# Two edits of one kernel: the first output product in nine blocks of 512 tokens, and attention bursts ahead of their tick's product

## The chip, the cores and the metric

The kernel runs on one core of a Trainium2 chip. The metric is the device time of one execution in microseconds (us), median of the runs shown. TensorE (PE) does the matmuls, VectorE (DVE), ScalarE (ACT) and GpSimd (POOL) the element-wise work, and SyncE (SP) issues every transfer, in one queue in the order of the program. Each engine works off its own instructions strictly in order.

## The reference

Three layers, one behind the other. Everything is float32, but the weights of the two feed-forward layers come as float64.

```python
# 1. retention: batch 8, heads 8, sequence 576, head size 64
scores = (q @ k.T) / sqrt(64)
attn = (scores * Dmat) @ v          # Dmat[i, j] = gamma_h ** (i - j) for i >= j, else 0
x = attn as [4608 tokens, 512]
# 2. maxout layer, width 768
h = maximum(maximum(x @ w1, x @ w2), x @ w3)
z = h @ w_out                       # [4608, 512]
# 3. bilinear layer, width 1024
g = (z @ w1') * (z @ w2')
out = (g @ w3') @ w_out'            # [4608, 512]
```

## The kernel before, in words

Every matmul of layers 2 and 3 is made of three: an operand is split into a high half that the fast float32r form holds exactly and a low half (`copy_r` on ACT makes the high half, `low` on DVE or POOL subtracts it), and high x high, low x high and high x low are summed in PSUM.

**Layers 1 and 2 in one stage.** The 4608 tokens are nine blocks of 512 (`N1`). Everything in this stage is put into a list with `when(t, fn)` and issued in the order of `t`; equal times keep the order of entry, and attention is entered ahead of the products. One block is 18 ticks (`T_BLK`): one product of 12 matmuls (`products`, L349, tile `ps_h`) at each tick k, entered at k - 0.5. Attention of one chunk of 64 or 128 tokens consists of the scores (`sc`, L263), the state's update (`st`, L288) and the outputs (`o`, L276 and L282), each in small float32 matmuls. For block t they are planned during block t - 1: outputs at `t_n`, the state's update 0.01 before, and the scores of the next chunk 0.01 after, with `t_n` = 18 (t - 1) - 0.5 + 18 i / (chunks in the block), which are four or five. So `t_n` falls on a product's time for the first chunk of a block, and for the third of four. At the same time the weights are turned from float64 and kept in DRAM. The first blocks' h goes to DRAM as `h_d`, one tensor for each block of 512.

**The first output product** (z = h @ w_out, tile `ps_z`, L506) works on blocks of 384 (`N2`), twelve of them. A block has six steps k; a step is 12 matmuls (four PSUM banks, three each) with one h tile (`hr` as loaded, `hh` and `hl` its halves), taken from the ring of `H_RING` tiles, and behind it in the program `split_h` prepares the tile two steps on and loads another (`load_h`; half of the loads come in two parts, since blocks of 384 and of 512 do not coincide). In four of the six steps one entry of `steps` is worked off: first the sums of weights for the next layer (L480, and splits), then weights for the w product. A block ends with four copies out of PSUM, two by ACT (L555) and two by DVE (L553), into one tile `zo`, which one DMA stores to `z_d`. The eight banks are two sets of four, so the next block runs while the copies are made.

**Then** come a product of two weights (`ps_w`), the bilinear layer (`ps_x`, `ps_v`, `ps_y`) in six pairs of 384-token blocks, which reads z back (`operands`, tile `zr`), and the last product.

Of the kernel before, what the change touches and what calls it, by code (L numbers as in the profile page):

```python
# [9 lines left out]
F32 = mybir.dt.float32  # L10
F32R = mybir.dt.float32r
I32 = mybir.dt.int32
U32 = mybir.dt.uint32
AF = mybir.ActivationFunctionType
# [5 lines left out]
NT, DM = B * S, H * D  # L20
F1, F2 = 768, 1024
G = H // 2
P = 128
N1 = 512
N2 = 384
KF1, KF2, KD = F1 // P, F2 // P, DM // P
# [43 lines left out]
def tile_retention_maxout_bilinear(ctx: ExitStack, tc, a, out):  # L70
    nc = tc.nc
    chunks = chunk_list()

    def copy_r(dst, src):
        nc.scalar.activation(dst, src, AF.Copy)  # L75

    def low(eng, dst, full, hi):
        eng.tensor_tensor(dst, full, hi.bitcast(F32), ALU.subtract)  # L78

    def load(dst, src):  # L80
        nc.sync.dma_start(out=dst, in_=src)  # L81
# [3 lines left out]
    dram = ctx.enter_context(tc.tile_pool(name="dram", bufs=1, space=DRAM))  # L85
# [2 lines left out]
    wo1_d = dram.tile([P, KF1, DM], F32, name="wo1_d")  # L88
    wp_d = dram.tile([P, 2, 2, KD, 512], F32, name="wp_d")
    h_d = [dram.tile([P, KF1, N1], F32, name=f"h_d{t}") for t in range(NT // N1)]  # L90
    z_d = [dram.tile([P, KD, N2], F32, name=f"z_d{t}") for t in range(NT // N2)]
    g_d = [dram.tile([P, KF2, N2], F32, name=f"g_d{t}") for t in range(NT // N2)]
    w4_d = dram.tile([P, KF2, DM], F32, name="w4_d")

# [21 lines left out]
    n_blk = NT // N1  # L116
    T_BLK = 3 * KF1
# [210 lines left out]
    for t, ns in by_block.items():  # L328
        for i, n in enumerate(ns):
            if t == 0:  # L330
                attend(n, CHUNK_AT[i], CHUNK_AT[i] + 2, CHUNK_AT[i] + 3)
            else:

                t_n = T_BLK * (t - 1) - 0.5 + T_BLK * i / len(ns)
                attend(n, behind + 0.01 if t > 1 else t_n - 3, t_n - 0.01, t_n)
                behind = t_n

# [28 lines left out]
    for t in range(n_blk):  # L366
        for f in range(KF1):
            for i in range(3):
                k = T_BLK * t + 3 * f + i
# [12 lines left out]
    zp = {}  # L382
    n2 = NT // N2
# [17 lines left out]
    def get_w1o(k):  # L401
        return splitter(zp["p"], wo1_d[:, k], *zp["w"][k], nc.vector if k % 2 else nc.gpsimd, "wr", 2)

    H_RING, H_AHEAD = 4, 4
    hq = dict(loaded=0, split=0)

    def load_h():
        n = hq["loaded"]
        if n < n2 * KF1:
            hq["loaded"] = n + 1  # L410
            j, k = divmod(n, KF1)
            raw = hq[n] = zp["p"].tile([P, N2], F32, tag="hr", name="hr", bufs=H_AHEAD)
            t0, done = j * N2, 0
            while done < N2:
                blk, off = divmod(t0 + done, N1)
                m = min(N1 - off, N2 - done)
                load(raw[:, done:done + m], h_d[blk][:, k, off:off + m])
                done += m

    def split_h():  # L420
        n = hq["split"]
        if n < n2 * KF1:
            hq["split"] = n + 1
            raw = hq.pop(n)
            hh = zp["p"].tile([P, N2], F32R, tag="hh", name="hh", bufs=H_RING)
            hl = zp["p"].tile([P, N2], F32R, tag="hl", name="hl", bufs=H_RING)
            copy_r(hh, raw)
            low(nc.vector if n % 2 else nc.gpsimd, hl, raw, hh)
            hq[n] = hh, hl
            load_h()  # L430
# [7 lines left out]
    for n in range(H_AHEAD):  # L438
        when(t_last + 11 + 0.5 * n, load_h)
    for n in range(2):  # L440
        when(t_last + 15 + n, split_h)

    with tc.manual_schedule():
# [7 lines left out]
        def bank8(name):  # L451
            return ps_8.tile([P, 512], F32, tag="b", name=name)
# [43 lines left out]
        steps = [groups[0][0]]  # L496
# [3 lines left out]
        def product(ps, terms, start=True, stop=True, again=False):  # L500

            mms = []
            for lh, ll, rh, rl in terms:
                mms += [(lh, rh), (ll, rh), (lh, rl)]
            for j, (l, r) in enumerate(mms):
                nc.tensor.matmul(ps, l, r, start=start and j == 0, stop=stop and j == len(mms) - 1, skip_group_check=again)  # L506
# [16 lines left out]
        def open_34():  # L523

            t34["p"] = t34x.enter_context(tc.tile_pool(name="t34", bufs=2, side="left"))
            gets = [lambda m=0, e=e: get_w3t(m, e) for e in range(2)] + [lambda k=k: get_wo2(k) for k in range(KF2)]
            gets += [lambda m=1, e=e: get_w3t(m, e) for e in range(2)]
            pending = []

            def step():  # L530
                if len(pending) == 3 or not gets:
                    pending.pop(0)()
                if gets:
                    pending.append(gets.pop(0)())

            return [step] * (len(gets) + 3)

        slots = (1, 2, 4, 5)
        for j in range(n2):
            zs = [bank8("ps_z") for _ in range(KD)]  # L540
            for k in range(KF1):
                h = hq.pop(j * KF1 + k)
                for m in range(KD):
                    ms = slice(m * P, (m + 1) * P)
                    wh, wl = zp["w"][k]
                    product(zs[m][:, :N2], [(wh[:, ms], wl[:, ms], *h)], k == 0, k == KF1 - 1)
                split_h()
                if k in slots and steps:
                    steps.pop(0)()
            zo = zp["p"].tile([P, KD, N2], F32, tag="zo", name="zo")  # L550
            for m in range(KD):
                if m % 2:
                    nc.vector.tensor_copy(zo[:, m], zs[m][:, :N2])  # L553
                else:
                    nc.scalar.activation(zo[:, m], zs[m][:, :N2], AF.Copy)  # L555
            load(z_d[j], zo)
            if j == n2 - 5:
                for step in steps:
                    step()
                sx.close()  # L560
                steps = open_34()
# [15 lines left out]
        def operands(pair, dst, c):  # L577

            w = {}

            def fetch():
                r = zr_p.tile([P, 2, 2, N2], F32, tag="zr", name="zr")
                for e in range(2):
                    for kk in range(2):
                        load(r[:, kk, e], z_d[2 * pair + e][:, 2 * kk + c])
                for e in range(2):
                    for kk in range(2):
                        w[f"b{kk + 1}{e + 1}"] = r[:, kk, e]

            def split(x, src, eng):  # L590
                h, l = dst[x]
                copy_r(h[:, c], w[src])
                low(eng, l[:, c], w[src], h[:, c])

            def sub(x, y, to=None):
                if to is None:
                    t = zr_p.tile([P, N2], F32, tag="t", name="t", bufs=2)
                else:
                    t = w[to]
                nc.vector.tensor_tensor(t, w[x], w[y], ALU.subtract)  # L600
                return t

            def first():
                split("b11", "b11", nc.gpsimd)
                w["t3"] = sub("b22", "b12")

            def second():
                split("b21", "b21", nc.gpsimd)
                w["t1"] = sub("b12", "b11", "b12")

            def third():
                split("b22", "b22", nc.gpsimd)
                w["t2"] = sub("b22", "t1")

            def fourth():
                split("t1", "t1", nc.vector)
                w["t4"] = sub("b21", "t2", "b21")

            def fifth():
                split("t2", "t2", nc.gpsimd)  # L620
                split("t3", "t3", nc.vector)

            return [fetch, first, second, third, fourth, fifth, lambda: split("t4", "t4", nc.gpsimd)]

        def waiting():
# [3 lines left out]
        steps = [halves[0][0], waiting] + halves[0][1:] + [halves[1][0], waiting] + halves[1][1:]  # L629
# [121 lines left out]
        def last_operands():  # L751


            def begin():
                opx.close()
                gpool[0] = last["t"] = ctx.enter_context(tc.tile_pool(name="ga", bufs=1, side="right"))

            w4s = [w4_steps(q) for q in range(2)]
            g = g_steps_late(0)
            return [begin, w4s[0][0], g[0], lambda: None, *g[1:]] + w4s[0][1:] + [lambda: (w4s[1][0](), second[0]())] + w4s[1][1:]  # L760
# [13 lines left out]
        for p in range(n_pair):  # L774
            B = ops[p % 2]
            steps = []
            if p + 1 < n_pair:
                nxt = ops[(p + 1) % 2]
                steps = operands(p + 1, nxt, 0) + operands(p + 1, nxt, 1)
            else:  # L780
                steps = last_operands()
# [140 lines left out]
```

## Time and profile before

| | us |
|---|---|
| median of 3 runs | 1372.39 (1371.77 to 1373.87) |
| the profiled execution | 1372.37 |
| its span, from the first to the last instruction | 1370.6 |
| PE busy in it | 1310.1 |
| DVE, POOL, ACT busy | 815.9, 503.8, 442.7 |

Read it by stages: PE is short of work only in the first 131 us and for some us around 1190. A matmul's busy time overlaps with its neighbours', so what a matmul costs is read from the length of an unbroken run divided by its number.

### The profile page before, as it was taken

How to read it: one execution, taken by the hardware profiler on the slowest of the kernel's cores; microseconds unless marked ns; L12 is line 12 of the kernel's file. 1: busy time of each engine (PE TensorE's matmuls, PEld its weight loads, DVE VectorE, ACT ScalarE, POOL GpSimd, SP SyncE). 2: the span in 40 equal slices, each digit the busy share in tenths (PEclk: the TensorE clock that was granted, in tenths of full speed). 3: DMA queues.
4: the chain of work that ended last, by engine and by line, in shares of the span. 5: the costliest groups of instructions: out<-in, count | busy, mean ns of one | idle time of the engine just before them, and what ended most of it. 6: DMA issues, size and time to landing. Idle time of an engine off the chain costs nothing.

```text
span 1370.6 us, 24656 instructions
## 1 busy us (share of the span) xinstructions
PE 1310.1 (96%) x9416; PEld 1191.0 (87%) x9416; DVE 815.9 (60%) x1205; ACT 442.7 (32%) x869; POOL 503.8 (37%) x433
## 2 busy tenths in 40 slices
PE   3787999999999999999999999999999999799998
PEld 2675888888888888889999989999999999799998
DVE  4999667757667677424663343343433336588885
ACT  1333212222221212113444333333333324355553
POOL 2642233323313232113653343343343435444442
PEclk7799999999999999999999999999999999999999
DMA  7866677777777788225656542222222231445452
GB/s 153 180 151 149 160 180 175 196 177 180 165 188 159 161 187 180 85 91 169 217 182 215 180 137 93 70 87 76 70 91 94 70 108 66 133 148 164 150 167 93
DMA packets 372519, 195.20 MB, mean 142 GB/s; under 512 B 267824, under 2 KB 346288, under 8 KB 372400
## 3 DMA queue, kind: packets, MB, share of 16 engines
q1 hardware_dynamic: 372400, 193.62, 52.8%
q8 instruction: 74, 1.21, 0.4%
q14 instruction: 45, 0.37, 0.1%
HBM read 127.49 MB, written 66.06 MB: 141 GB/s over the span
## 4 chain that ended last, share of the span: by engine, by line
PE 89%; DVE 1%; DMA 1%; issue 1%; SPq 1%; ACT 0%; POOL 0%; DVEq 0%; ACTq 0%; POOLq 0%
PE ps_h L349 31%; PE ps_x L506 21%; PE ps_z L506 11%; PE ps_y L506 11%; PE ps_v L506 5%; PE ps_w L506 3%; PE o L276 2%; PE sc L263 2%; PE st L288 1%; PE o L282 1%; SPq L81 1%; DMA gr<-g_d 0%; DMA raw<-in_moe_w_dram 0%; DVE w L700 0%; DVE gr L737 0%
## 5 line engine op out<-in xcount | busy, mean ns | idle before, releaser
L349 PE MATMUL ps_h<-xh,w1h 128*128 128x512 f32 (+1 forms) x672 | 264.6, 396 | 8.3 <-ACT w1h L75 3.4
L349 PE MATMUL ps_h<-xh,w1l 128*128 128x512 f32 (+1 forms) x672 | 258.5, 387 | 1.3 <-POOL w1l L78 1.2
L142 POOL TENSOR_TENSOR l<-l,e 128x512 f32<-128x512 f32 x55 | 70.8, 1288 | 319.0 <-DVE e L141 241.5
L349 PE MATMUL ps_h<-xl,w1h 128*128 128x512 f32 (+1 forms) x672 | 176.4, 385 | 2.3 <-DVE xl L78 2.3
L349 PEld LDWEIGHTS ps_h<-xh,w1h 128*128 128x128 f32 x672 | 128.4, 191 | 42.0 <-issue 7.3
L349 PEld LDWEIGHTS ps_h<-xh,w1l 128*128 128x128 f32 x672 | 128.4, 191 | 26.0 <-POOL w1l L78 2.3
L349 PEld LDWEIGHTS ps_h<-xl,w1h 128*128 128x128 f32 x672 | 125.1, 190 | 27.5 <-DVE xl L78 2.5
L801 POOL TENSOR_TENSOR c<-c 128x384 f32<-128x384 f32 x72 | 81.6, 1133 | 171.2 <-DVE c L670 83.2
L665 ACT ACTIVATE snap<-ps_x 128x384 f32<-128x384 f32 x120 | 58.7, 491 | 197.7 <-PE ps_x L506 195.5
L360 DVE TENSOR_TENSOR hb<-ps_h,hb 128x512 f32<-128x512 f32 (+1 forms) x112 | 74.1, 663 | 65.7 <-PE ps_h L349 63.0
L134 ACT ACTIVATE e<-raw 128x512 f32<-128x512 f32 x64 | 42.9, 670 | 191.4 <-DMA raw<-in_moe_w_dram 153.6
L506 PE MATMUL ps_z<-hh,w1oh 128*128 128x384 f32 x288 | 96.3, 334 | 0.8 <-issue 0.8
L506 PE MATMUL ps_z<-hl,w1oh 128*128 128x384 f32 x288 | 96.2, 334 | 0.0
L506 PE MATMUL ps_z<-hh,w1ol 128*128 128x384 f32 x288 | 96.2, 334 | 0.0
L75 ACT ACTIVATE hb<-ps_h 128x512 f32<-128x512 f32 (+1 forms) x56 | 32.4, 578 | 157.9 <-PE ps_h L349 152.0
L146 DVE TENSOR_TENSOR m<-m,l 128x512 f32<-128x512 f32 x64 | 62.0, 969 | 23.4 <-POOL l L142 23.3
L270 DVE TENSOR_TENSOR p<-sc,tables 128x512 f32<-128x512 f32 (+1 forms) x80 | 46.9, 626 | 40.1 <-PE sc L263 40.0
L78 POOL TENSOR_TENSOR hl<-hr,hh 128x384 fp32r<-128x384 f32 x36 | 39.4, 1093 | 78.2 <-ACT hh L75 75.8
L263 PE MATMUL sc<-qt,kt 64*64 64x128 f32 (+1 forms) x1152 | 43.3, 281 | 22.3 <-DVE kt L256 20.5
L670 DVE TENSOR_TENSOR c<-ps_v,snap 128x384 f32<-128x384 f32 x48 | 26.7, 557 | 62.1 <-PE ps_v L506 40.1
L256 DVE STREAM_TRANSPOSE qt<-q 128x512 f32<-128x512 f32 (+1 forms) x40 | 38.6, 964 | 40.0 <-POOL q L249 28.3
L263 PEld LDWEIGHTS sc<-qt,kt 64*64 64x64 f32 x1152 | 35.4, 142 | 28.3 <-issue 16.2
(213 smaller groups left out, 3493.7 us busy)
## 6 DMA issues: line engine op xcount, KB each, us to landing
g_d<-c SPq DMA_DIRECT2D x96, 192.0 KB, 1.9
raw<-in_moe_w_dram SPq DMA_DIRECT2D x34, 512.0 KB, 4.9
h_d<-hb SPq DMA_DIRECT2D x54, 256.0 KB, 3.1
gr<-g_d SPq DMA_DIRECT2D x12, 1024.0 KB, 6.2
z_d<-zo SPq DMA_DIRECT2D x12, 768.0 KB, 3.6
zr<-z_d SPq DMA_DIRECT2D x48, 192.0 KB, 3.3
out_dram<-ob SPq DMA_DIRECT2D x36, 256.0 KB, 2.0
q<-in_q_dram SPq DMA_DIRECT2D x128, 64.0 KB, 3.5
```

The lines of the kernel that those rows point to most:

```text
L78: eng.tensor_tensor(dst, full, hi.bitcast(F32), ALU.subtract)
L134: nc.scalar.activation(z["e"], raw[:, :, 1].bitcast(F32), AF.Copy, scale=2.0 ** -112)
L142: eng.tensor_tensor(z["l"], z["l"], z["e"], ALU.mult)
L146: nc.vector.tensor_tensor(m, m, z["l"], ALU.add)
L256: nc.vector.transpose(out=z[x + "t"][:, :, :c].rearrange("p h (t T) -> p T h t", T=r), in_=z[x][:, :r])
L263: nc.tensor.matmul(z["sc"][g][keys, h, :c], z["kt"][rows, h, keys], z["qt"][rows, h, :c], start=True, stop=True)
L270: nc.vector.tensor_tensor(z[g][:c, :, :c], z["sc"][g][:c, :, :c], mask[:c, :c].unsqueeze(1).to_broadcast([c, G, c]), ALU.mult)
L349: nc.tensor.matmul(ps[:, cols], l, r, start=n == 0, stop=n == len(mms) - 1)
L360: nc.vector.tensor_tensor(hb, ps[:, cols], hb, ALU.max)
L506: nc.tensor.matmul(ps, l, r, start=start and j == 0, stop=stop and j == len(mms) - 1, skip_group_check=again)
L665: nc.scalar.activation(t, ps[:, :N2], AF.Copy)
L801: nc.gpsimd.tensor_tensor(x, x, y, ALU.mult)
```

## The change

**Planner.** `t_n` is 0.02 earlier, so that scores, state update and outputs of a chunk all come before the product of a tick on which it falls. All other times that hang on `t_n` move by the same 0.02.

**First output product.** Blocks of 512 in place of 384: nine blocks of the same six steps; h tiles of 512 columns, always loaded in one part; rings of three in place of four split tiles; the weight steps at every k, in the first five blocks except k = 0. `zo` becomes a tile for two banks, used twice in a block from the same buffer, with a store each. z is kept in blocks of 512, so that `operands` reads some of its tiles in two parts.

```diff
-    z_d = [dram.tile([P, KD, N2], F32, name=f"z_d{t}") for t in range(NT // N2)]
+    z_d = [dram.tile([P, KD, N1], F32, name=f"z_d{t}") for t in range(NT // N1)]
...
-                t_n = T_BLK * (t - 1) - 0.5 + T_BLK * i / len(ns)
+                t_n = T_BLK * (t - 1) - 0.52 + T_BLK * i / len(ns)
                 attend(n, behind + 0.01 if t > 1 else t_n - 3, t_n - 0.01, t_n)
...
-    H_RING, H_AHEAD = 4, 4
+    H_RING, H_AHEAD = 3, 4
...
-            raw = hq[n] = zp["p"].tile([P, N2], F32, tag="hr", name="hr", bufs=H_AHEAD)
-            t0, done = j * N2, 0
-            while done < N2:
-                blk, off = divmod(t0 + done, N1)
-                m = min(N1 - off, N2 - done)
-                load(raw[:, done:done + m], h_d[blk][:, k, off:off + m])
-                done += m
+            raw = hq[n] = zp["p"].tile([P, N1], F32, tag="hr", name="hr", bufs=H_AHEAD)
+            load(raw, h_d[j][:, k])
...
-        slots = (1, 2, 4, 5)
-        for j in range(n2):
+        for j in range(n_blk):
...
-                    product(zs[m][:, :N2], [(wh[:, ms], wl[:, ms], *h)], k == 0, k == KF1 - 1)
+                    product(zs[m], [(wh[:, ms], wl[:, ms], *h)], k == 0, k == KF1 - 1)
                 split_h()
-                if k in slots and steps:
+                if steps and (k or j > 4):
                     steps.pop(0)()
-            zo = zp["p"].tile([P, KD, N2], F32, tag="zo", name="zo")
-            for m in range(KD):
-                if m % 2:
-                    nc.vector.tensor_copy(zo[:, m], zs[m][:, :N2])
-                else:
-                    nc.scalar.activation(zo[:, m], zs[m][:, :N2], AF.Copy)
-            load(z_d[j], zo)
-            if j == n2 - 5:
+            for m in range(0, KD, 2):
+                zo = zp["p"].tile([P, 2, N1], F32, tag="zo", name="zo")
+                nc.scalar.activation(zo[:, 0], zs[m], AF.Copy)
+                nc.vector.tensor_copy(zo[:, 1], zs[m + 1])
+                load(z_d[j][:, m:m + 2], zo)
+            if j == n_blk - 4:
...
-                        load(r[:, kk, e], z_d[2 * pair + e][:, 2 * kk + c])
+                        t0, done = (2 * pair + e) * N2, 0
+                        while done < N2:
+                            blk, off = divmod(t0 + done, N1)
+                            m = min(N1 - off, N2 - done)
+                            load(r[:, kk, e, done:done + m], z_d[blk][:, 2 * kk + c, off:off + m])
+                            done += m
```

How the instructions stand now is shown at three places. On PE, at the third chunk of a block of four during the second block of products, before (the outputs' last matmuls with the old state `s`, one product, the first scores):

```order
L282 MATMUL o<-qt,s 64x128 x8
L349 MATMUL ps_h<-xh,w1h_122 128x512
L349 MATMUL ps_h<-xh,w1l_128 128x512
L349 MATMUL ps_h<-xh,w1h_122 128x512
L349 MATMUL ps_h<-xh,w1l_128 128x512
L349 MATMUL ps_h<-xh,w1h_122 128x512
L349 MATMUL ps_h<-xh,w1l_128 128x512
L349 MATMUL ps_h<-xh,w1h_122 128x512
L349 MATMUL ps_h<-xh,w1l_128 128x512
L349 MATMUL ps_h<-xl,w1h_122 128x512 x4
L263 MATMUL sc_1791<-qt,kt 64x128
L263 MATMUL sc_1792<-qt,kt 64x128
```

and of the changed kernel, from the last outputs on:

```order
L276 MATMUL o<-p_1659,v 64x128
L276 MATMUL o<-p_1661,v 64x128
L282 MATMUL o<-qt,s 64x128 x8
L263 MATMUL sc_1775<-qt,kt 64x128
L263 MATMUL sc_1776<-qt,kt 64x128
```

The twelve matmuls of the product have moved behind the scores.

On SP, in the first 130 us, from the fetch of the last unit of the layer-2 weights (`raw<-in_moe_w_dram`) on, before:

```order
L81 DMA raw<-in_moe_w_dram 128x4x256
L81 DMA h_d_64<-hb 128x512
L81 DMA v<-in_v_dram 128x8x64
L81 DMA kn<-in_k_dram 128x8x64
L81 DMA raw<-in_moe_w_out_dram 128x1024
L81 DMA h_d_64<-hb 128x512
L81 DMA q<-in_q_dram 32x16x32 x4
L81 DMA k<-in_k_dram 32x16x32 x4
```

and of the changed kernel:

```order
L81 DMA raw<-in_moe_w_dram 128x4x256
L81 DMA h_d_64<-hb 128x512
L81 DMA v<-in_v_dram 128x8x64
L81 DMA kn<-in_k_dram 128x8x64
L81 DMA q<-in_q_dram 32x16x32 x4
L81 DMA k<-in_k_dram 32x16x32 x4
L81 DMA raw<-in_moe_w_out_dram 128x1024
L81 DMA h_d_64<-hb 128x512
```

The eight fetches of q and k have moved ahead of the fetch of w_out and of a store of h.

On DVE, at the end of the first block of the first output product (`hl` is the low half of an h tile, `s` a sum of weights, COPY the copies out of PSUM), before:

```order
L480 TENSOR_TENSOR s_6572<-s_6530,a_6501 128x512
L78 TENSOR_TENSOR hl<-hr,hh 128x384
L553 COPY zo<-ps_z 128x384 x2
L78 TENSOR_TENSOR hl<-hr,hh 128x384
L480 TENSOR_TENSOR s_6651<-a_6501,a_6505 128x512
```

and of the changed kernel:

```order
L475 TENSOR_TENSOR s_6546<-s_6524,a_6496 128x512
L78 TENSOR_TENSOR hl<-hr,hh 128x512
L475 TENSOR_TENSOR s_6594<-a_6496,a_6500 128x512
L547 COPY zo<-ps_z 128x512 x2
L78 TENSOR_TENSOR hl<-hr,hh 128x512
```

The sum of weights that stood behind the block's copies has moved in front of them.

## Rows read from the trace of the kernel before

**Rows 1.** The page: span, busy time of the engines, chain by engine.

```profile
span 1370.6 us, 24656 instructions
...
PE 1310.1 (96%) x9416; PEld 1191.0 (87%) x9416; DVE 815.9 (60%) x1205; ACT 442.7 (32%) x869; POOL 503.8 (37%) x433
...
PE 89%; DVE 1%; DMA 1%; issue 1%; SPq 1%; ACT 0%; POOL 0%; DVEq 0%; ACTq 0%; POOLq 0%
```

**Rows 2.** Windows: length, busy time by engine, granted clock, DMA share, GB/s.

```profile
131.00:564.40 433.40, 433.38 (x3644) 349.49 (x3644) 305.40 (x485) 95.64 (x165) 128.81 (x119) 0.99 0.74 171
...
625.30:775.30 150.00, 149.94 (x865) 149.97 (x866) 76.05 (x88) 65.60 (x132) 73.58 (x60) 1.00 0.61 196
775.30:818.90 43.60, 43.60 (x194) 36.08 (x193) 17.84 (x19) 16.68 (x34) 19.43 (x16) 1.00 0.53 169
```

**Rows 3.** The chain from 158 to 206 us: start, us, what.

```profile
171.92 0.61 PE st L288 x16
...
174.01 2.94 PE ps_h L349 x12
176.96 1.03 PE sc L263 x32
177.99 11.15 PE ps_h L349 x48
189.14 0.62 PE st L288 x16
...
191.22 0.87 PE sc L263 x32
192.10 11.10 PE ps_h L349 x48
203.20 0.62 PE st L288 x16
```

**Rows 4.** The chain over the whole span: three unbroken runs of matmuls.

```profile
564.46 60.06 PE ps_h L349 x264
625.36 150.00 PE ps_z L506 x864
775.36 43.56 PE ps_w L506 x192
```

**Rows 5.** The chain near 130 us, and SP's timeline there (last row).

```profile
121.95 5.30 DMA raw<-in_moe_w_dram
...
131.02 4.21 PE ps_h L349 x9
...
124.62 3.21 SPq L81 DMA_DIRECT2D raw<-in_moe_w_out_dram  x1
```

**Rows 6.** Timeline at the ninth block's end: ACT, DVE, SP; idle before in brackets.

```profile
736.39 0.49 ACT L555 ACTIVATE zo<-ps_z 128x384 f32<-128x384 f32 x1 [1.73 <-PE ps_z L506]
...
736.91 0.56 DVE L553 COPY zo<-ps_z 128x384 f32<-128x384 f32 x1 [2.18 <-PE ps_z L506]
737.95 0.56 DVE L553 COPY zo<-ps_z 128x384 f32<-128x384 f32 x1 [0.48 <-PE ps_z L506]
...
738.57 0.32 SPq L81 DMA_DIRECT2D z_d<-zo  x1
```

**Rows 7.** Operations on 512 columns: ns min/median/max, or count, busy us and mean ns.

```profile
L360 DVE TENSOR_TENSOR hb<-ps_h,hb x112: 408/684/692, 54.8 to 624.6; 128x512 f32<-128x512 f32 x104, 128x256 f32<-128x256 f32 x8
...
L75 ACT ACTIVATE oh<-raw 128x512 fp32r<-128x512 f32 x8 | 4.9, 618 | 0.0
...
L78 POOL TENSOR_TENSOR ol<-raw,oh 128x512 fp32r<-128x512 f32 x4 | 5.2, 1289 | 3.1 <-ACT oh L75 3.1
...
L480 DVE TENSOR_TENSOR s<-a,a 128x512 f32<-128x512 f32 x8 | 9.6, 1196 | 8.0 <-DMA a<-wp_d 8.0
```

**Rows 8.** Transfers: KB each, median us to landing; and the z stores' spread.

```profile
z_d<-zo SPq DMA_DIRECT2D x12, 768.0 KB, 3.6
...
out_dram<-ob SPq DMA_DIRECT2D x36, 256.0 KB, 2.0
...
DMA to landing us min/median/max: 3.3/3.6/6.6
```

More of the change, by code (lines that the diff above doesn't have):

```diff
@@ L408, in load_h @@
         n = hq["loaded"]
-        if n < n2 * KF1:
+        if n < n_blk * KF1:
             hq["loaded"] = n + 1
             j, k = divmod(n, KF1)
-            raw = hq[n] = zp["p"].tile([P, N2], F32, tag="hr", name="hr", bufs=H_AHEAD)
-            t0, done = j * N2, 0
-            while done < N2:
-                blk, off = divmod(t0 + done, N1)
-                m = min(N1 - off, N2 - done)
-                load(raw[:, done:done + m], h_d[blk][:, k, off:off + m])
-                done += m
+            raw = hq[n] = zp["p"].tile([P, N1], F32, tag="hr", name="hr", bufs=H_AHEAD)
+            load(raw, h_d[j][:, k])
     def split_h():
         n = hq["split"]
-        if n < n2 * KF1:
+        if n < n_blk * KF1:
             hq["split"] = n + 1
             raw = hq.pop(n)
-            hh = zp["p"].tile([P, N2], F32R, tag="hh", name="hh", bufs=H_RING)
-            hl = zp["p"].tile([P, N2], F32R, tag="hl", name="hl", bufs=H_RING)
+            hh = zp["p"].tile([P, N1], F32R, tag="hh", name="hh", bufs=H_RING)
+            hl = zp["p"].tile([P, N1], F32R, tag="hl", name="hl", bufs=H_RING)
             copy_r(hh, raw)
```

## The prediction

> **What bounds the kernel now.** I read the page's head and the chain of waits by engine first: TensorE is busy 1310.1 of 1370.6 us and holds 89% of the chain [rows 1]. The windows by stage then say where that is tight. From 131 us to 564 us TensorE is busy 433.38 of 433.40 us, in the first output product 149.94 of 150.00 us; in the latter stage VectorE, ScalarE and GpSimd work 76.0, 65.6 and 73.6 us [rows 2]. So in both stages that the change touches every nanosecond that TensorE spends counts, and the other engines have about half of their time to spare on average. What can go wrong there is a single late operand, not a load. The third view, the chain in order of time, gives the two prices: what a turn from one kind of matmul to the other costs, and what a matmul of 384 and of 512 columns costs [rows 3, 4].
>
> The profiled execution took 1372.37 us, its span 1370.6; the median of the three runs is 1372.39, so the sum is made against 1372.4.
>
> **The bursts (the planner's -0.5 becoming -0.52).** Where a chunk falls on a tick, its outputs now stand before that tick's product and the next chunk's scores behind it; with -0.52 the scores stand in front too, as the rows of the order show. A chunk that falls between two ticks was in one burst already. Of the places where outputs, twelve product matmuls and scores follow one another there are twelve in the order, eleven of them behind 131 us.
>
> Price of one, both forms from one stretch [rows 3]: divided, from the state update at 171.92 to the next one at 189.14, it takes 17.22 us, with 12 + 48 product matmuls in it. In one burst, from 189.14 to 203.20, it takes 14.06 us with 48. A product matmul in an undisturbed run takes 60.06/264 = 0.2275 us [rows 4], so 12 more make 2.73 and the sum 16.79 us. The difference is 0.43 us. Nothing is left out of the work: what goes is one exit from the product and one entry into it. Of the eleven, some are smaller (chunks of 64 tokens, and first chunks that have no old state to add), so I take 0.40 each: **-4.4 us**. Bounds: nothing if the turn costs the same wherever it stands, 11 x 0.43 = 4.7.
>
> The cover for the earlier scores: their operands must be there one product, 2.73 us, sooner. The trace has bursts of this very form, with the scores directly behind the outputs, and no gap in them [rows 3]; should an operand be late, each would cost up to that 2.73 us.
>
> The Trainium skill, TensorEngine Tiling (Array Packing), Key Properties, says that a change of tiling mode drains TensorE. By that rule two changes of mode go at each of the places; the trace agrees with a price of 0.43 us for the two.
>
> **What moves at the start.** The same -0.02 lets fetches of q and k pass others in the order of SyncE's queue. One place is on the chain. The last unit of first weights is issued at 121.95 and lands 5.30 us later, and TensorE waits for what is made of it until 131.02. Behind it the queue stood at the w_out fetch from 124.62 for 3.21 us, and the q and k fetches came after that; now they come before it and share the DMA engines with the weights that TensorE waits for [rows 5]. Bounds: nothing, and 1.5 us (half of the eight transfers of 64 KB, 256 KB, at the 171 GB/s of [rows 2]). I take **+0.6 us**. The twelfth burst lies here, where a saving only lengthens this wait, so I count it at nothing.
>
> **Nine blocks of 512 for twelve of 384.** 864 matmuls take 150.00 us, 173.6 ns each; 512 columns in the next product take 43.56/192 = 226.9 ns [rows 4]. 648 of these make 147.0 us: **-3.0 us**. The columns are the same 331,776; per matmul some 13 ns go with their number. Bounds: with the product's 227.5 ns, 147.4; nothing lower is shown.
>
> The Trainium skill, TensorE: Matmul & The Clock Gate, Back-to-back issue gap, puts the part that does not grow with the columns at about 2.5 ns. By that rule the 216 matmuls fewer would save an estimated 0.5 us. The two rows differ by 53.3 ns for 128 columns, which leaves 13.7 ns, so the measurement decides against it here.
>
> The fetches of h become 54 in place of 108 parts; the later reads of z become 72 in place of 48, in a stage in which TensorE is not waiting for them. Both I count at nothing: what hides the reads is the w product between, 43.6 us.
>
> **The new wait.** Output tiles were one of four banks, now two of two banks in one buffer. The second pair of copies must wait until the store of the first pair has landed, and behind those copies stand, on ScalarE, the split of the third h tile of the next block, then its low half on GpSimd, then TensorE. By the clock of one boundary, counted from the block's end E:
>
> Before, block nine ends at 625.36 + 9 x 12.50 = 737.86. ScalarE's first copy starts at 736.39 and VectorE's at 736.91, each 0.09 us behind its bank (9 and 6 matmuls before E); SyncE issues the store 0.06 us after the last copy [rows 6]. With matmuls of 0.227 us the banks are ready at E-2.04 and E-1.36, VectorE copies 512 in 0.68 us [rows 7], so the store leaves at E-0.53. Its 512 KB lie between 256 KB in 2.0 us and 768 KB in 3.6 us [rows 8]: 2.8, so it lands at E+2.3. Then a copy (0.62), the split (0.62) and the low half (1.29) [rows 7]: E+4.8. TensorE takes the third h tile at 24 x 0.227 = 5.45 and its low half at 5.90. Spare: 1.1 us, no wait.
>
> But in four of the eight boundaries (the rows of VectorE show the first) a sum of weights now stands between VectorE's last split and its first copy. The split of the previous tile starts at E-2.63, ends at E-2.0, its low half about E-1.1, the sum (1.20 in the mean [rows 7]) E+0.1, the copy E+0.8, the landing E+3.65, and the low half E+6.2: 0.3 us late, more where GpSimd slows the sum. I take 0.5 in each, and 0.4 more for the one that meets a fetch of four weight pieces: **+2.4 us**. Bounds: nothing, and, if every store took the slowest one's 6.6 us [rows 8], 2.7 x 8 = 21.6.
>
> **Sum:** 1372.4 - 4.4 + 0.6 - 3.0 + 2.4 = **1368.0 us**.
>
> **Rivals.**
> *No new waits at all*: landing always under 3.9 us and the sums out of the way, and the start unmoved: 1372.4 - 4.4 - 3.0 = 1365.0. For it: 1.1 us of spare; against: the order of VectorE.
> *The waits eat the gain*: stores of 4.4 to 5.1 us at all boundaries make 0.5 to 1.2 us each, 4 to 9.6 in sum, and the time 1369.6 to 1372.4 or a little over; say 1371.0. For it: before, the median store of 768 KB took 3.6 us, but others up to 6.6.
> *Slower*, by the same buffer: from a landing of 5.2 us at all eight boundaries on, where the waits pass the gains. At 5.8 it is 8 x 1.9 = 15.2 us, so 1372.4 - 4.4 + 0.6 - 3.0 + 15.2 = 1380.8. Against it: 512 KB would have to take longer than the median 768 KB.
> The Trainium skill, Trainium Kernel Development and Optimization, Best Practices, asks for double buffers so that DMA and compute overlap; here one buffer, smaller than before, is filled twice in a block. By that rule it is this rival; the trace gives 1.1 us of cover to set against it.
> *The bursts give nothing*, the turn costing as much in one burst as in two: 1372.4 + 0.6 - 3.0 + 2.4 = 1372.4. Against it stand the two forms in [rows 3].
>
> **How the numbers follow.** A measurement of this kernel can tell about 0.2%, 2.7 us, from no change: faster is below 1369.7, slower above 1375.1. Forecast (1366.5 to 1369.7): 0.50. No new waits (under 1366.5): 0.17. Waits eat the gain: 0.20. Bursts give nothing: 0.08. Slower: 0.05. So faster 0.67, same 0.28, slower 0.05. The range reaches from the first rival to the middle of the second, 1364.8 to 1371.2; the upper part of the second rival, the last two and a little below are left out.
>
> **What the profile of the changed kernel would show.** Bursts: in the chain no more runs of 12 product matmuls, runs of 60 in their place, and the first output product starting about 3.8 us sooner than 625.36. Matmuls: 648 at 226.9 ns. New wait: ScalarE and VectorE idle before their second copies until a DMA, and TensorE idle before a low half in three to five boundaries, 0.3 to 1 us each; the stage from the first of these matmuls to the w product 149.4 us. Start: the weights' landing a little over 5.30 us. It would be wrong above all through the landing time of the store and through how long VectorE's sum takes beside GpSimd.

## The result, and the profile after

| us | before | after |
|---|---|---|
| median (4 runs each) | 1372.08 | 1381.15 |
| lowest and highest | 1370.87 to 1373.87 | 1378.98 to 1381.38 |
| first output product starts at | 625.36 | 620.64 |
| from its start to that of the w product | 150.00 | 163.77 |
| from there to the end of the span | 595.2 | 594.9 |

The changed kernel is slower: ratio 1.0058, interval 1.0046 to 1.0071, 8 us by the ratio and 9.1 us between the medians, where 4.4 us of gain were forecast. The three lower rows come from the chains over the whole span, of the kernel before [rows 4] and of the changed one:

```profile
620.64 16.58 PE ps_z L501 x72
...
784.41 43.56 PE ps_w L501 x192
```

The differences, -4.7, +13.8 and -0.3 us, make the 8.7 us by which the span grew. So what stands ahead of the first output product gained, and the product lost three times as much.

The page's head of the changed kernel:

```profile
span 1379.3 us, 24123 instructions
...
PE 1310.2 (95%) x9200; PEld 1165.0 (84%) x9200; DVE 821.0 (60%) x1190; ACT 437.9 (32%) x845; POOL 507.1 (37%) x424
```

And its windows, columns as in [rows 2]: two stages, the first output product by block (the second block in two rows), and a stretch of the second block once more, finer:

```profile
131.00:559.80 428.80, 428.44 (x3644) 349.93 (x3645) 307.28 (x485) 94.78 (x165) 129.76 (x119) 1.00 0.75 174
...
620.60:784.20 163.60, 153.60 (x648) 122.74 (x649) 78.31 (x73) 60.43 (x108) 75.26 (x51) 0.98 0.52 175
...
620.60:637.05 16.45, 16.41 (x73) 13.62 (x73) 5.72 (x6) 5.21 (x9) 7.56 (x5) 1.00 0.47 153
637.05:648.00 10.95, 6.63 (x28) 4.87 (x27) 3.03 (x4) 2.78 (x6) 1.39 (x3) 0.95 0.69 224
648.00:661.11 13.11, 13.11 (x47) 10.54 (x47) 8.65 (x8) 4.88 (x9) 8.18 (x6) 0.78 0.33 105
661.11:677.95 16.84, 16.62 (x74) 13.43 (x72) 9.10 (x11) 7.26 (x13) 9.11 (x6) 1.00 0.65 219
677.95:694.27 16.32, 16.32 (x74) 13.51 (x72) 9.83 (x10) 6.74 (x12) 8.95 (x6) 1.00 0.59 201
694.27:711.48 17.21, 16.63 (x74) 13.42 (x73) 10.44 (x9) 7.67 (x14) 11.91 (x8) 1.00 0.49 174
711.48:730.63 19.15, 17.20 (x73) 13.28 (x72) 11.17 (x10) 6.73 (x12) 8.29 (x6) 1.00 0.41 141
730.63:748.60 17.97, 16.90 (x73) 13.36 (x72) 4.82 (x6) 6.33 (x11) 6.86 (x5) 1.00 0.65 218
748.60:766.35 17.75, 16.91 (x74) 13.36 (x72) 8.80 (x8) 7.89 (x14) 8.54 (x6) 1.00 0.70 236
766.35:784.20 17.85, 16.87 (x73) 13.35 (x72) 6.74 (x6) 4.94 (x9) 4.47 (x4) 1.00 0.24 89
...
641.50:646.40 4.90, 1.16 (x7) 0.62 (x5) 0.69 (x1) 1.18 (x3) 0.00 (x0) 1.00 0.47 178
646.40:652.50 6.10, 5.52 (x13) 4.07 (x14) 5.33 (x4) 2.99 (x6) 4.39 (x3) 0.54 0.61 215
```

TensorE has as much busy time as before, and between 131 and 560 us it is still busy for all but 0.4 us. In the first output product it lacks 10 us, and even its busy time there, 153.6 us, is above the 147.0 of 648 matmuls.

An unbroken block is 72 x 0.227 = 16.3 us. The second takes 24.06, 7.7 too long; the others from the third on 0.5, 0, 0.9, 2.8, 1.6, 1.4 and 1.5. Sum 16.4. What TensorE waited for, by the view of its waits in this stage (us in total, times, the longest):

```profile
PE ps_z L501 <- ACT hh L75: 5.1, 5, 3.7
PE ps_z L501 <- POOL hl L78: 3.9, 7, 0.7
PE ps_z L501 <- DVE hl L78: 0.9, 1, 0.9
```

Halves of h tiles, then. The timelines of SyncE and ScalarE tell what those stood behind: SyncE's row of z_d is the issue of a block's two stores (the first's start, and the time to the end of the second; ahead of the first boundary's stand four weight pieces and an h tile), ScalarE's the first of the second pair of copies, with its wait.

```profile
635.83 1.96 SPq L81 DMA_DIRECT2D a<-wp_d  x4
637.88 0.41 SPq L81 DMA_DIRECT2D hr<-h_d  x1
638.41 7.90 SPq L81 DMA_DIRECT2D z_d<-zo  x2
...
662.14 3.79 SPq L81 DMA_DIRECT2D z_d<-zo  x2
...
677.54 4.33 SPq L81 DMA_DIRECT2D z_d<-zo  x2
...
730.23 6.37 SPq L81 DMA_DIRECT2D z_d<-zo  x2
...
748.88 5.48 SPq L81 DMA_DIRECT2D z_d<-zo  x2
```

```profile
645.22 0.60 ACT L546 ACTIVATE zo<-ps_z 128x512 f32<-128x512 f32 x1 [9.23 <-DMA z_d<-zo]
645.71 1.14 ACT L75 ACTIVATE hh<-hr 128x512 fp32r<-128x512 f32 x2
...
664.84 0.60 ACT L546 ACTIVATE zo<-ps_z 128x512 f32<-128x512 f32 x1 [4.79 <-DMA z_d<-zo]
...
680.78 0.60 ACT L546 ACTIVATE zo<-ps_z 128x512 f32<-128x512 f32 x1 [3.89 <-DMA z_d<-zo]
...
735.51 0.60 ACT L546 ACTIVATE zo<-ps_z 128x512 f32<-128x512 f32 x1 [6.12 <-DMA z_d<-zo]
...
753.25 0.60 ACT L546 ACTIVATE zo<-ps_z 128x512 f32<-128x512 f32 x1 [5.70 <-DMA z_d<-zo]
```

From a store's issue to the copy that waits for it these five boundaries show 6.8, 2.7, 3.2, 5.3 and 4.4 us; the copy starts 8.2, 3.7, 2.8, 4.9 and 4.7 us after the block's end. The other three boundaries, not shown here, have 3.6, 2.7 and 4.3 us, and their copies start 4.1, 4.8 and 4.8 us after the block's end. By the forecast's clock a copy may start 2.3 + 1.1 = 3.4 us after it. Only the 2.8 keeps that, and the block behind it is the one without a wait.

The first boundary, by the timelines of VectorE, then of TensorE:

```profile
635.90 1.77 DVE L475 TENSOR_TENSOR s<-a,a 128x512 f32<-128x512 f32 x1
637.60 0.68 DVE L547 COPY zo<-ps_z 128x512 f32<-128x512 f32 x1
```

```profile
646.39 0.50 PE L501 MATMUL ps_z<-hh,w1oh 128*128 128x512 f32 x1 [3.74 <-ACT hh L75]
...
648.34 0.63 PE L501 MATMUL ps_z<-hh,w1oh 128*128 128x512 f32 x1
648.77 0.63 PE L501 MATMUL ps_z<-hh,w1ol 128*128 128x512 f32 x1
```

The sum of weights holds VectorE's copy until 637.60, 0.55 us after the block's end; the four weight pieces (1 MB) and the h tile were issued from 635.83 on, just ahead of the store, which lands after 6.7 us; TensorE stands still for 3.74 us, and then its matmuls follow one another every 0.43 us in place of 0.227. The windows show the granted clock with it: 0.78 of full speed from 648.00 to 661.11.

### The profile page after: what moved, and what is told of

The parts are those of the page before. It is cut to its first block, busy times and chain, and to the rows that moved or that the text cites. A ratio compares the mean times of both kernels' runs of the same rounds, so it can differ in the third digit from the quotient of the medians.

```text
span 1379.3 us, 24123 instructions
## 1 busy us (share of the span) xinstructions
PE 1310.2 (95%) x9200; PEld 1165.0 (84%) x9200; DVE 821.0 (60%) x1190; ACT 437.9 (32%) x845; POOL 507.1 (37%) x424
## 4 chain that ended last, share of the span: by engine, by line
PE 83%; issue 4%; DVE 3%; DMA 1%; POOL 1%; SPq 1%; ACT 1%; POOLq 0%; DVEq 0%; ACTq 0%
PE ps_h L349 29%; PE ps_x L501 21%; PE ps_y L501 11%; PE ps_z L501 7%; PE ps_v L501 5%; PE ps_w L501 3%; PE o L276 2%; PE sc L263 2%; PE st L288 1%; PE o L282 1%; SPq L81 1%; POOL hl L78 1%; DMA raw<-in_moe_w_dram 1%; DMA gr<-g_d 0%; DVE w L697 0%
## 5 line engine op out<-in xcount | busy, mean ns | idle before, releaser
L501 PE MATMUL ps_z<-hh,w1oh 128*128 128x512 f32 x216 | 85.8, 397 | 5.9 <-ACT hh L75 5.1
L501 PE MATMUL ps_z<-hl,w1oh 128*128 128x512 f32 x216 | 86.2, 399 | 4.9 <-POOL hl L78 3.9
L501 PE MATMUL ps_z<-hh,w1ol 128*128 128x512 f32 x216 | 85.2, 394 | 0.0
L78 POOL TENSOR_TENSOR hl<-hr,hh 128x512 fp32r<-128x512 f32 x27 | 38.9, 1445 | 84.6 <-ACT hh L75 84.6
L148 DVE SCALAR_TENSOR_TENSOR w<-raw,m 128x512 int32<-128x512 int32 x64 | 59.0, 922 | 2.7
```

The lines of the kernel that those rows point to most:

```text
L148: nc.vector.scalar_tensor_tensor(w, z["hi"], -0x80000000, z["m"], ALU.bitwise_and, ALU.bitwise_or)
```

## Experiments

Each run is compared with runs of the kernel before that were taken with it; their medians lie between 1372.24 and 1373.60 us.

Theory A: the lost time is the wait for the first store's landing, through the one buffer that is filled twice and the splits that stand behind the waiting copy on ScalarE. Theory B: the splits are late by themselves, since a weight step now stands at every step and tiles of 512 take longer. Theory C, for the first boundary alone: the stage's first store is slow of itself (one of its stores took 6.6 us before, [rows 8]).

**The bursts alone.** The kernel before with one line:

```diff
-                t_n = T_BLK * (t - 1) - 0.5 + T_BLK * i / len(ns)
+                t_n = T_BLK * (t - 1) - 0.52 + T_BLK * i / len(ns)
```

> The kernel before with the planner's edit alone (-0.52 for -0.5). Theory: in the changed kernel the first product started 4.72 us sooner (620.64 against 625.36), and all of that is from the bursts; alone they give 1372.1 - 4.7 = 1367.4 us, with the start of the first product near 620.6 and that product still 150.0 us. Rival: part of the 4.7 us comes from the other edit (h in 512 blocks changes nothing before the first product, so this would have to be the order of transfers); then less than 4 us is left, 1368.1 or more.

1367.42 us against 1373.44, ratio 0.9956 (0.9945 to 0.9968): a gain of 6.0 us, with 4.4 to 7.6 for its interval. The first output product starts at 621.79 and takes its old 150.03 us, by the chain:

```profile
172.44 0.62 PE st L288 x16
...
560.90 60.06 PE ps_h L349 x264
621.79 150.03 PE ps_z L506 x864
```

From this state update to the long run it is 388.46 us, where [rows 3, 4] have 564.46 - 171.92 = 392.54: 4.1 us for the ten divided bursts between, 0.41 each. Whether the rest of the 6.0 us is a gain of the edit or chance is not shown.

**The blocks alone.** The changed kernel with -0.5 put back.

> The changed kernel with the planner's -0.5 put back, so the nine blocks alone. Theory: the first product took 163.6 us in place of 150.0, so alone it costs 13.6 us: 1372.1 + 13.6 = 1385.7 us. Rival: the two edits are not independent, and the waits of the first product come from transfers that the bursts had moved; then the stage is shorter than 163 us and the time below 1383.

1383.24 us, ratio 1.0071 (1.0059 to 1.0083), that is some 9.7 us above the kernel before. The time lies between the two sides; the stage is 161 us long, under 163, as the rival had it. Here the block that starts at 733.8 had no wait, where its like in the changed kernel lost 1.6 us, and the second block lost 6.8 us in place of 7.7. Whether the bursts do that, or the waits differ from one execution to the next, is open, since each kernel has one profile. What is shown is that the waits are there without the bursts.

**Two buffers for zo**, in the place of the two in which this product's weights had been loaded:

```diff
...
-                zo = zp["p"].tile([P, 2, N1], F32, tag="zo", name="zo")
+                zo = zp["p"].tile([P, 2, N1], F32, tag="zo", name="zo", bufs=2)
```

> The changed kernel with two buffers for the output tile zo (the second takes the place of the buffer in which the weights of this product were loaded), all instructions and stores as they were. Theory (the second pair of copies waits for the first pair's store, and with it all that stands behind on ScalarE): the waits go, the product takes 648 x 0.227 = 147.0 us in place of 163.6, and the kernel 1381.2 - 16.6 = 1364.6 us; the granted clock stays at 1.00 in the second block. Rival (the h tiles are late because weight steps now stand at every step and their splits are 512 wide, in rings of three): TensorE waits as before, 1378 us or more.

1366.15 us, ratio 0.9943 (0.9931 to 0.9955). The window of the stage:

```profile
623.67:770.68 147.01, 147.01 (x648) 121.78 (x649) 62.59 (x73) 62.09 (x109) 68.40 (x51) 1.00 0.60 195
```

No wait, clock 1.00, with every weight step, split and ring as in the changed kernel: theory B falls. Its stores took 2.6 to 7.1 us to land, and no matmul waited for them.

**Two buffers without the bursts.**

> Nine blocks with two buffers for zo, but the planner's -0.5 of before. Theory: what is left is 648 matmuls of 0.227 us for 864 of 0.1736 us, 147.0 us in place of 150.0: 3.0 us below the kernel before, ratio 0.998. Rival (512-wide blocks give nothing, the whole gain of the version with two buffers is the bursts'): ratio 1.000 within its interval, stage 150 us.

1370.01 us against 1373.60, ratio 0.9977 (0.9967 to 0.9987); the stage is 147.01 us again. The nine blocks of 512 are worth their 3.0 us.

**The second use of the buffer without the 512.** The kernel before with its blocks of 384:

```diff
-            zo = zp["p"].tile([P, KD, N2], F32, tag="zo", name="zo")
...
-            load(z_d[j], zo)
+            for m in range(0, KD, 2):
+                zo = zp["p"].tile([P, 2, N2], F32, tag="zo", name="zo")
...
+                load(z_d[j][:, m:m + 2], zo)
```

> The kernel before (blocks of 384, the old planner) with zo as a tile of two banks, filled twice in a block from one buffer, and a store for each. Theory (the cost is the buffer's second use, not the 512): the next block's third h tile is wanted 24 x 0.1736 = 4.2 us after a block's end and its low half 4.5 us after it, and landing, copy, split and low half (0.49 + 0.5 + 1.02 us) come in front of it, so landings of 2.6 to 6.7 us make some 0.5 to 4 us at each of eleven boundaries: the stage grows by 10 to 25 us, 1383 to 1398 us. Rival (the waits come from splits and rings of 512 columns): the stage stays near 150 us, 1374 us.

1398.62 us, ratio 1.0179 (1.0164 to 1.0193), just above the range expected. The windows of the stage and of its second and fourth blocks:

```profile
625.76:802.82 177.06, 160.64 (x865) 154.53 (x866) 86.11 (x88) 62.96 (x131) 80.83 (x60) 0.96 0.52 166
638.32:657.46 19.14, 14.51 (x73) 13.68 (x73) 10.35 (x9) 6.28 (x13) 8.59 (x6) 0.91 0.52 158
...
670.52:690.01 19.49, 15.80 (x73) 14.98 (x73) 8.72 (x10) 6.28 (x13) 8.55 (x6) 0.82 0.51 167
```

The buffer's second use alone, in a kernel without any 512-wide tile in this stage, costs 27 us there.

**The weight step between the copies.** The step of a block's last k is issued between the two pairs of copies:

```diff
-                if steps and (k or j > 4):
+                if steps and k < KF1 - 1 and (k or j > 4):
...
                 load(z_d[j][:, m:m + 2], zo)
+                if m == 0 and steps:
+                    steps.pop(0)()
```

> The changed kernel with the weight step of a block's last step issued between the two pairs of copies in place of in front of them. Theory: the first store leaves 0.41 us before the block's end at all boundaries (it left 0.3 to 2.1 us after it at six of the eight), so the waits shrink by what the store was late: those at the end of blocks 1, 2, 5 (7.7, 0.5, 0.9 us with what follows them) by 1.2 to 2.5 each as far as they reach, blocks 7 and 8 by 0.7 to 0.9 each; block 6 keeps its 2.8, and block 1 some 3 of wait, since four weight pieces stay ahead of its store. 1372 to 1376 us. Rival (dense steps alone make the waits, the store's landing does not count): all waits go, 1365 us. Second rival (the landing sets it, and the hour at which the store leaves is nothing beside the transfers ahead of it): less than 3 us gained, 1378 us or more.

1377.05 us against 1373.44, ratio 1.0023 (1.0015 to 1.0032): below the changed kernel, but at the upper edge of what was expected. The third block lost its wait, as expected, the second kept more than expected (two blocks' windows):

```profile
638.18:660.78 22.60, 18.24 (x74) 14.36 (x72) 11.41 (x12) 7.77 (x14) 9.52 (x8) 0.92 0.55 176
660.78:677.10 16.32, 16.32 (x74) 13.52 (x72) 8.11 (x10) 7.37 (x13) 8.28 (x7) 1.00 0.66 225
```

So VectorE's late first copy, which makes the store late, is a part of it. At the first boundary it is not what decides: there the second block still lost 6.3 us, and the store still stood behind the weight pieces and took 6.2 us to land.

**The weight pieces behind the store.**

```diff
-                if steps and (k or j > 4):
+                if steps and (k or j > 4 or j in (1, 2)) and (j or k < 4):
```

> The changed kernel with the second fetch of four weight pieces (1 MB) issued behind the stores of the first block, not in front of them, and the sum of weights that stood in front of that block's copies gone from there too (the steps run through blocks 1 and 2 at every k instead). Theory (the first store lands 6.7 us after its issue because the pieces lie ahead of it in the queue, and TensorE's clock falls behind the wait): the second block runs without a wait at a clock of 1.00, which gives back its 7.7 us: 1381.2 - 7.7 = 1373.5 us, the ratio to the kernel before 1.000; the boundaries from 5 on as they were. Rival (the stage's first store is slow of itself, as it was in the kernel before): the second block keeps its wait, 1380 us or more.

1374.95 us against 1373.60, ratio 1.0007 (0.9997 to 1.0017), as theory A has it. The second block's window is

```profile
638.27:654.84 16.57, 16.57 (x73) 13.44 (x72) 11.15 (x9) 7.66 (x14) 10.41 (x7) 1.00 0.70 234
```

with no wait and an undisturbed clock. Theory C falls: the slowest store of this kernel lands in 4.4 us, so the first one is not slow when no weight pieces lie just ahead of it. In the kernel before, the store that took 6.6 us had four of them just ahead of it too (SyncE's timeline):

```profile
637.91 1.97 SPq L81 DMA_DIRECT2D a<-wp_d  x4
639.99 0.40 SPq L81 DMA_DIRECT2D z_d<-zo  x1
```

(This edit takes the sum of weights away from this boundary too; in the run above, where the step with the sum went behind the first pair of copies and the pieces stayed ahead of the store, the second block lost 6.3 of its 7.7 us.)

**One-bank tiles.** The same 4096 bytes as two tiles of one bank, four stores of 256 KB:

```diff
-            for m in range(0, KD, 2):
-                zo = zp["p"].tile([P, 2, N1], F32, tag="zo", name="zo")
...
+            for m in range(KD):
+                zo = zp["p"].tile([P, N1], F32, tag="zo", name="zo", bufs=2)
...
+                load(z_d[j][:, m], zo)
```

> The changed kernel with the same 4096 bytes of zo cut into two tiles of one bank, four stores of 256 KB in a block in place of two of 512 KB. Theory (what counts is when ScalarE's second copy may start): its store is issued as soon as ScalarE's own first copy is done, about 1.3 us before the block's end, so even a landing of 4 us leaves the h tiles in time; only the first boundary, with the weight pieces ahead of the store, waits, 1 to 5 us. 1366 to 1371 us. Rival (a small buffer used more often waits more often): four uses in a block instead of two, each with a landing of its own, 1381 us or more.

1378.00 us, ratio 1.0032 (1.0020 to 1.0044): neither range was met. What failed is the forecast of when the store leaves and how soon it lands. At the first boundary, 638.97, the store could go at -1.1 us and went at +1.3, since SyncE was issuing what stands ahead of it (its timeline):

```profile
637.73 1.96 SPq L81 DMA_DIRECT2D a<-wp_d  x4
639.79 0.41 SPq L81 DMA_DIRECT2D hr<-h_d  x1
640.30 8.15 SPq L81 DMA_DIRECT2D z_d<-zo  x4
```

And a store of half the size hardly lands sooner: from issue to landing the median is 2.8 us for these 256 KB and 2.7 for the 512 KB of the changed kernel, and the quickest took 2.3 and 2.6 us.

**The second pair of copies one step later, and two steps later**, with the one buffer:

```diff
...
+                if late and k == 1:
+                    late.pop()(2)
...
-            for m in range(0, KD, 2):
+            def pair(m, j=j, zs=zs):
...
+            pair(0)
+            late.append(pair)
+            if j == n_blk - 1:
+                late.pop()(2)
```

(k == 1 is two steps, k == 0 one.) One step later the third h tile's split stands ahead of the waiting copy, two steps later the fourth's too.

> The changed kernel, one buffer for zo, with the second pair of copies (and its store) issued one step later: behind the split of the next block's third h tile and that step's weight step. Theory (the waiting copy costs time only through what stands behind it on ScalarE): the third tile is no longer late; the fourth, now behind the copies, is wanted 36 x 0.227 = 8.2 us after the block's end, and landing, copy, split and low half stay under that but at the first boundary, where the copies began 8.2 us after the end: some 2 us are left there, nothing elsewhere. 1364.6 + 2 = 1366 to 1368 us by the first comparison's 1372.1, ratio 0.995 to 0.997. Rival (the second use of the buffer costs whatever the order, because SyncE's queue stands at the second store and the loads of h behind it come late): 1375 us or more.

> The same, two steps later: behind the splits of the third and the fourth h tile. Theory: no wait is left, the product takes 147.0 us with one buffer as with two, and the ratio to the kernel before is that of the version with two buffers, 0.994. Rival (loads of h late behind the second store in SyncE's queue): the waits move to a later step of the block, ratio above 0.998.

1367.12 us against 1372.24, ratio 0.9964 (0.9952 to 0.9976), and 1364.83 us, ratio 0.9944 (0.9932 to 0.9957). The windows of the stage, of the first and then of the second:

```profile
619.32:767.48 148.16, 147.87 (x648) 121.50 (x649) 80.15 (x73) 60.53 (x108) 77.56 (x51) 1.00 0.58 194
```

```profile
621.00:767.97 146.97, 146.97 (x648) 121.74 (x649) 66.34 (x73) 61.73 (x108) 70.12 (x51) 1.00 0.59 195
```

One step leaves 1.1 us, two leave nothing. In the second one the buffer is as small, the stores land after up to 8.2 us, and the copies still wait for them; what no longer stands behind the waiting copy are the splits of the next block's third and fourth h tiles. Both this version and the one with two buffers beat the kernel before by some 7.7 us.

## Why the prediction was wrong

*The bursts, -4.4*: right in its price. Eleven at 0.40 were forecast, and ten of them measured 0.41 each. Alone, the edit gained 6.0 us, with the forecast's 4.4 at the lower end of the interval.

*The start, +0.6*: not settled. In the changed kernel the chain indeed runs there through SyncE's queue, and ends on a fetch of k that has moved ahead of the w_out fetch:

```profile
124.71 2.92 SPq L81
...
131.75 2.42 DMA k<-in_k_dram
...
138.59 2.79 PE ps_h L349 x11
```

But between the kernels tried, whatever their edits, the state update near 172 us starts between 169.9 and 173.5, which is more than the term.

*The blocks, -3.0*: right, 147.0 us in every version without waits. The Trainium skill, TensorE: Matmul & The Clock Gate, Back-to-back issue gap, gives a fixed part of about 2.5 ns for an isolated matmul, from which an estimated 0.5 us would have come; the trace does not agree, with stages of 147.01 and 150.0 us.

*The new wait, +2.4*: this is the step that failed; the time that it cost is 16.6 us. Its place, its chain (store, copy, split, low half) and its clock were right, and the time allowed to the copy, 3.4 us after the block's end, separates the blocks with a wait from the one without. The forecast's last sentence had named the two sizes that failed, the landing and the sum. What it put in was wrong in three ways.
1. *The landing.* I took 2.8 us from between the medians of 256 and 768 KB, as if the size decided. The median in the changed kernel is 2.7, so that number was met and was still the wrong one: the median is over both stores of a block, and only the first counts, which meets weights and h tiles in the queue: from its issue to the copy that waits it took 2.7 to 6.8 us at the eight boundaries. The stores of [rows 8] had a maximum of 6.6 beside their 3.6, and what that store stood behind was in the trace. I priced the boundary with four weight pieces at 0.4 us more; it cost 7.7.
2. *The issue.* The store was late: at four boundaries VectorE's copy was held back by sums of weights, by 0.9 to 2.5 us, and at two others SyncE issued a fetch first. The sum took 1.77 to 1.79 us at the three of the four where GpSimd was at work for most of it, and 0.68 at the one where GpSimd stood; the mean of 1.20 that the forecast used is neither. The four stood in the order, and I gave them 0.5 us each.
3. *The clock.* A wait of 3.7 us was followed by matmuls at 0.43 us. No term stood for that. Of the second block's 7.7 us, some 2.9 are this, by an estimate from the trace: about fourteen matmuls at 0.2 us more. No run takes the clock apart from the wait.

The outcome is the rival called *Slower*, whose example gave 1380.8 us; only the waits were not eight alike but seven, one of them of 7.7 us. That the example lies so near the measurement is luck: it had the store take 5.8 us at all eight boundaries, and at one alone did the copy wait longer than that. Its chance of 0.05 was set by the argument that 512 KB would have to take longer than the median of 768 KB. Two of the rivals' sums were off besides: stores of 5.1 us at all boundaries give 1365.6 + 9.6 = 1375.2, not 1372.4 or a little over, and the waits pass the gains from 4.8 us on, not from 5.2. The sum with the measured term, and without the start, is 1372.1 - 4.4 - 3.0 + 16.6 = 1381.3, for 1381.15; that is closer than runs of 1378.98 to 1381.38 can tell.

The Trainium skill, Trainium Kernel Development and Optimization, Best Practices, spoke for that rival with its advice to double-buffer. The runs agree, with 147.0 us for the stage in place of 163.6, and add that one buffer costs nothing either when no operand that is wanted soon stands behind the copy that waits.

## What to carry to other kernels

When a change makes an engine wait for a transfer, don't price the transfer by its size and a median: list what its queue holds at that moment, and take the spread. Then look at what stands behind the waiting instruction on its engine: to move two splits ahead of it gave as much as a second buffer. And a gap in TensorE's work can cost more than its length: in the second block a wait of 3.74 us was followed by matmuls at 0.43 in place of 0.227 us.

## What was not expected of the hardware

Between 256 and 512 KB the time from issue to landing hardly depended on the size of these stores: with one buffer, or with four small stores in a block, the medians were 2.8 us for 256 KB, 2.6 for 384 and 2.6 to 2.9 for 512, against 3.6 and 3.7 for 768 (with two buffers for zo, where one store follows close behind the other, 3.7 and 3.8 for 512). But in every kernel in which a store comes just behind four weight pieces (1 MB) the slowest took 6.1 to 8.2 us. In the one kernel whose stores do not, it was 4.4. After the wait of 3.74 us the granted clock was 0.54 of full speed from 646.40 to 652.50, so for nearly all of that time it was at the lower of the two levels, 1.2 GHz; from 661.11 on it was 1.00 again in every block.
